# Two pairs of attention and GEGLU layers on one core: filling work given out by a running sum, and the second slot's gate moved from step 11 to step 9

## The chip, the cores and the metric

The kernel runs on one core of a Trainium2 chip. The metric is the time of one execution on the device in microseconds (us), as the median of several runs. The engines are named as in the profile: PE (TensorE, matrix products), DVE (VectorE), ACT (ScalarE), POOL (GpSimd) and SP (SyncE, which issues most transfers here).

## The reference

An input x of 2048 rows by 512 columns goes through four layers, each added to x: attention, feed-forward, attention, feed-forward. Cut to what matters:

```python
x = x + attention(layernorm(x)); x = x + ffn(layernorm(x))
x = x + attention(layernorm(x)); x = x + ffn(layernorm(x))

def attention(x):            # 32 heads of width 16, 4 segments of 512 rows, in order
    q, k, v = x @ wq, x @ wk, x @ wv            # each 512 x 512
    for s in range(4):
        p = softmax(q_s @ k_s.T / 4 + causal_mask)
        a_dot = p @ v_s
        a_mem = (phi(q_s) @ M) / (phi(q_s) @ z + 1e-6)   # phi(t) = t + 1 if t > 0, else exp(t)
        o_s = g * a_mem + (1 - g) * a_dot                 # g = sigmoid(beta), per head
        M = M + phi(k_s).T @ v_s;  z = z + phi(k_s).sum(0)
    return o @ wo

def ffn(x):                  # w_gate, w_up: 512 x 1792, w_down: 1792 x 512
    return (gelu(x @ w_gate) * (x @ w_up)) @ w_down
```

## The kernel before, in words

The work is cut into eight attention units (two attention layers of four segments each) and eight feed-forward units. The program runs through eight slots, k = 0 to 7. In slot k the softmax part of attention unit k is worked in 20 steps, t = 0 to 19 (the loop calls them steps; the title of the change calls them pairs). Around these steps lies everything else, as filling work for PE.

A step (function scores) does 4 or 8 small products of queries and keys (tile st in PSUM, two buffers, each holding two banks), then two exponentials on ACT (pt from st, 128 x 1024 each), then masks on POOL (line 368). Steps with t mod 5 equal to 1, 2 or 4 have 8 products, the others 4. The next step's products write the same two st buffers, so they wait for this step's exponentials. After steps with t mod 5 = 2 or 4 a block of 40 small products with v falls due one step later (function flush, tile ps_q, line 394); it reads the masked pt.

The filling of slot k is a list of items, each with a cost written by hand in us: 0.87 for four 512-wide products, 1.52 for seven of them, and so on. In slots 1 to 7 the list has two parts. The first (pre) is the memory part of unit k (den, four num, upd), the output projection wo of unit k-1 in four pieces (wo0 to wo3), the down projection of feed-forward unit k-2 in eight halves (d00, d01 to d30, d31), and the first half of the q and k projections of unit k+1 (q0, k0, q1, k1). After wo1 and after wo3 the layer norm of two row tiles each is started; it runs over DVE (add, statistics), POOL (lines 156 and 159: ve and rs), DVE again (xn, line 161) and SP (transposes of xn into xnT). Then comes the gate of feed-forward unit k-1: 56 products (tile psg, line 438) and seven Gelus on ACT, in one piece with no steps between. It needs all of xnT, and uses the st buffers. Before it ACT loads the table of the Gelu, and after it the table of the exponential. The second part (post) is the up projection in 14 items (u0 to u13, line 446), q2, k2, q3, k3 and the v projection v0 to v3 of unit k+1. Slot 0 has no gate: its list is its own v, q and k, the v, q and k of unit 1, upd, two loads and two layer norms. It alone cuts each step in two and runs filling also between the halves.

The orders of PE, ACT and SP are those in which the program is written. Those of DVE and POOL are set by a scheduler. All fillings, den and num too, and the flushes take their PSUM from one pool of four buffers (tag m). What q and k leave to do on ACT (an exponential e for phi) and v on ACT (a copy) is deferred until after the exponentials of the next step.

Before the change, the filling of a step is counted down: budget = remaining cost / remaining steps, items are run while less than the budget is spent, half of it (0.5) ahead of the flush and the rest behind it. An item that overshoots the budget is run whole. In the part ahead of the gate 1.7 us are held back (GATE_LEAD), and 1.7 us of the second part are run at once behind it (GATE_TAIL).

Of the kernel before, what the change touches and what calls it, by code (L numbers as in the profile page):

```python
# [31 lines left out]
STEPS = 4 * PAIRS  # L32
FLUSH_LAG = 1
G_STEP = 11
G_FIRST = 11
GATE_LEAD = 1.7
GATE_TAIL = 1.7
ST_BUFS = 2
# [4 lines left out]
def kernel(  # L43
# [39 lines left out]
    def load_x(sgi):  # L83
        nc.sync.dma_start(out=x_sb[:, TPS * sgi:TPS * (sgi + 1), :], in_=xv[:, TPS * sgi:TPS * (sgi + 1), :])

    def load_w(w_sb, w):
        nc.sync.dma_start(out=w_sb[:], in_=w.rearrange("(kt p) n -> p kt n", p=P))
# [11 lines left out]
                            fill=1.0, base=0, channel_multiplier=1)  # L99
# [3 lines left out]
                            fill=0.0, base=0, channel_multiplier=1)  # L103
    nc.gpsimd.affine_select(out=bd[:], in_=bd[:], pattern=[[16, 8], [0, 16]], compare_op=ALU.is_ge,
                            fill=0.0, base=15, channel_multiplier=-1)
# [17 lines left out]
    def late_constants():  # L123
        nc.vector.tensor_scalar(out=cden[:], in0=tmp_e[:], scalar1=1.0, scalar2=None, op0=ALU.add)
        for i in range(2):
            va = cst.tile([P, TPS, H, DH + 1], BF16, name=f"vaug{i}")
            nc.vector.tensor_copy(out=va[:, :, :, DH], in_=cden[:].unsqueeze(1).to_broadcast([P, TPS, H]))
            vaugs.append(va)
        nc.vector.tensor_scalar(out=tmp_e2[:], in0=tmp_e2[:], scalar1=1.0, scalar2=None, op0=ALU.add)
        nc.vector.reciprocal(out=gvec[:], in_=tmp_e2[:])  # L130
        for b in range(4):
            nc.vector.tensor_tensor(out=bdg[:, b, :].rearrange("p (h e) -> p h e", e=16),
                                    in0=bd[:].rearrange("p (h e) -> p h e", e=16),
                                    in1=gvec[:, 8 * b:8 * b + 8].unsqueeze(2).to_broadcast([P, 8, 16]),
                                    op=ALU.mult)
# [46 lines left out]
    def run_deferred():  # L182
        while deferred:
            deferred.pop(0)()
# [299 lines left out]
    fill = []  # L484
    clock = [0]

    def run_fill(budget):
        spent = 0.0
        while fill and spent < budget:
            c, fn = fill.pop(0)  # L490
            fn()
            spent += c
            while len(deferred) > 2:
                deferred.pop(0)()
        return spent

    def flush_due(force=False):
        while pending and (force or pending[0][0] <= clock[0]):
            _, u, b, par, pts = pending.pop(0)
            u.flush(b, par, pts)  # L500
            if (b, par) == (3, 1):
                u.turn()

    def merge(a, b):
        outl, na, nb = [], len(a), len(b)
        ia = ib = 0
        while ia < na or ib < nb:
            if ib >= nb or (ia < na and ia * nb <= ib * na):
                outl.append(a[ia]); ia += 1
            else:  # L510
                outl.append(b[ib]); ib += 1
        return outl

    with tc.manual_schedule(engines={ENG.PE, ENG.Activation, ENG.SP}):
        ln0 = LN(0)
        for j in range(TPS):
            ln0.stats(j)
        x0T = ln0.by_pe()
        late_constants()
        qk0, v0 = att[0].stage_a(lambda: x0T)  # L520
        for c, fn in qk0[:2]:
            fn()
            run_deferred()
        for i in range(1, NSEG):
            a_ln[i] = LN(TPS * i)

        def ln_items(i, with_stats):
            items = [(0.0, lambda j=j: a_ln[i].stats(j)) for j in range(TPS)] if with_stats else []
            return items + [(0.0, lambda: a_ln[i].by_dma())]

        for k in range(2 * NSEG):
            A = att[k]
            nxt_qk, nxt_v = [], []
            if k + 1 < 2 * NSEG:
                nxt_qk, nxt_v = att[k + 1].stage_a(lambda k=k: a_ln[k + 1].xnT)
            upd = A.mem_update() if A.s < NSEG - 1 else []
            if k == 0:
                pre = (v0 + qk0[2:4] + ln_items(1, True) + qk0[4:] + nxt_v + nxt_qk[0::2] + upd
                       + [(0.0, lambda: load_x(3)), (0.0, lambda: load_w(wd_sb, B_w_down))]
                       + ln_items(2, True) + nxt_qk[1::2])  # L540
                post, F, g_at = [], None, STEPS
            else:
                F = ffn[k - 1]
                f_ln = LN(F.tt0)
                wo_prev = att[k - 1].wo(f_ln)
                wo_prev = (wo_prev[:2] + [(0.0, lambda f_ln=f_ln: f_ln.by_dma(0, 2))] + wo_prev[2:]
                           + [(0.0, lambda f_ln=f_ln: f_ln.by_dma(2, 2))])
                pre = (A.mem() if A.s > 0 else []) + upd
                if k == 1:
                    pre += nxt_qk[:2] + wo_prev + nxt_qk[2:4]  # L550
                    g_at = G_FIRST
                else:
                    Fp, ln_d = ffn[k - 2], None
                    if Fp.lyr == 1:
                        ln_d = a_ln[NSEG + Fp.c] = LN(Fp.tt0)
                    down_prev = Fp.down(ln_d)
                    pre += down_prev[:4] + merge(wo_prev + down_prev[4:], nxt_qk[:4])
                    g_at = G_STEP
                post = merge(F.up(), nxt_qk[4:] + nxt_v)
                if k + 2 < 2 * NSEG:  # L560
                    post = merge(post, ln_items(k + 2, k + 2 < NSEG))
            fill[:] = pre
            for t in range(STEPS):
                if t == g_at:
                    run_fill(1e9)
                    run_deferred()
                    F.gate(f_ln.xnT)
                    fill[:] = post
                    run_fill(GATE_TAIL)
                left = (g_at if t < g_at else STEPS) - t  # L570
                if t < g_at <= STEPS - 1:
                    budget = max(0.0, sum(c for c, _ in fill) - GATE_LEAD) / left
                else:
                    budget = sum(c for c, _ in fill) / left
                budget -= 1e-6
                if k == 1 and 4 <= t < 8:
                    budget = max(budget, 1.74)
                if k == 0:
                    budget = max(budget, 1.0)
                    part = []  # L580
                    got = A.scores(t, between=lambda: part.append(run_fill(0.45 * budget)))
                    budget -= part[0]
                else:
                    got = A.scores(t)
                run_deferred()
                clock[0] += 1
                if got:
                    pending.append((clock[0] + FLUSH_LAG, A, *got))
                budget -= run_fill(0.5)
                flush_due()  # L590
                run_fill(budget)
            run_fill(1e9)


        F = ffn[-1]
        f_ln = LN(F.tt0)
        wo = att[-1].wo(f_ln)
        down_prev = ffn[-2].down(None)
        fill[:] = down_prev[:2]
        run_fill(1e9)  # L600
        flush_due(force=True)
        fill[:] = down_prev[2:5] + wo + down_prev[5:]
        run_fill(1e9)
        run_deferred()
        F.gate(f_ln.by_pe())
        for c, fn in F.up() + F.down(None):
            fn()
# [30 lines left out]
```

## Time and profile before

| | |
|---|---|
| median of 3 runs | 649.8 us (649.67 to 650.47) |
| the profiled execution | 648.93 us, span 647.2 us |
| mean granted PE clock | 0.965 |
| PE busy | 600.8 us (93%) |
| ACT busy | 426.2 us (66%) |
| DVE busy | 388.1 us (60%) |
| POOL busy | 221.4 us (34%) |

The span is the time from the first to the last instruction of the profile; 1.7 us of the execution lie outside it. Matmuls are pipelined and their ends are modelled, so starts are the firmer numbers. In the timeline a row reads: start, length, engine, line, operation, tile written<-tiles read, shape, count, and in brackets the idle time ahead and what ended it. The rows that matter stand in the prediction.

### The profile page before, as it was taken

To read this page: it belongs to the slowest core of one execution; us is meant where nothing else is said; L and a number is where in the kernel's file an instruction comes from. 1 tells how busy PE (TensorE), PEld (TensorE's weight loads), DVE (VectorE), ACT (ScalarE), POOL (GpSimd) and SP (SyncE) were. 2 spreads that over 40 slices of the span, in tenths; PEclk is the share of its full clock that TensorE was granted. 3 is DMA by queue.
4 is the path that set the end of the run, shared out by engine and by line. 5 is a ranking of instruction groups with operands and counts; after the bars stand their busy time and mean duration, and the time that the engine had idled before them with its cause. 6 is when DMAs were issued, how large, how long until landed. Compare 5 with 4: busy or idle time off the path is not lost.

```text
span 647.2 us, 14327 instructions
## 1 busy us (share of the span) xinstructions
PE 600.8 (93%) x5856; PEld 284.9 (44%) x5856; DVE 388.1 (60%) x917; ACT 426.2 (66%) x474; POOL 221.4 (34%) x505
## 2 busy tenths in 40 slices
PE   3997786999999999999999999999999999989997
PEld 1343543445444544444454454445444444434443
DVE  5897395467847568364756588386654546144352
ACT  2588785785767767675777858587676877572420
POOL 1434453143523445142432435133431445042000
PEclk9798595999999999998999999999999999999999
DMA  8945021021120012101130012210210012001001
GB/s 291 205 147 92 10 50 25 1 50 35 24 44 2 2 34 51 32 17 34 27 57 11 10 33 43 41 18 12 49 42 1 2 43 46 13 1 44 23 0 33
DMA packets 70578, 27.42 MB, mean 42 GB/s; under 512 B 61552, under 2 KB 69488, under 8 KB 70512
## 3 DMA queue, kind: packets, MB, share of 16 engines
q1 hardware_dynamic: 70368, 26.49, 18.1%
q8 instruction: 46, 0.75, 0.5%
q14 instruction: 20, 0.16, 0.1%
q10 hardware_dynamic: 144, 0.01, 0.0%
HBM read 9.71 MB, written 2.10 MB: 18 GB/s over the span
## 4 chain that ended last, share of the span: by engine, by line
PE 68%; ACT 12%; issue 8%; DVE 7%; POOL 3%; DMA 1%; SPq 0%; POOLq 0%; ACTq 0%
PE psg L438 15%; PE psu L446 13%; ACT pt L359 11%; PE psd L462 11%; PE st L352 9%; PE ps_q L394 7%; PE ps L206 5%; PE ps L247 4%; PE pso L419 2%; DMA x_sb<-in_A_x_dram 1%; DVE st L147 1%; POOL pt L368 1%; POOL rs L159 1%; DVE x_sb L422 1%; DVE xn L161 1%
## 5 line engine op out<-in xcount | busy, mean ns | idle before, releaser
L359 ACT ACTIVATE pt<-st 128x1024 bf16<-128x1024 f32 x320 | 310.4, 1024 | 107.3 <-PE st L352 103.5
L368 POOL TENSOR_SCALAR_AFFINE_SELECT pt<-pt 128x256 bf16<-128x256 bf16 (+1 forms) x448 | 195.5, 452 | 334.3 <-ACT pt L359 327.4
L449 DVE TENSOR_TENSOR gel<-gel,psu 128x512 bf16<-128x512 bf16 x112 | 76.3, 685 | 139.6 <-PE psu L446 136.2
L446 PE MATMUL psu<-xnT,wu_sb 128*128 128x512 bf16 x448 | 111.8, 380 | 0.0
L462 PE MATMUL psd<-wd_sb,gel 128*128 128x512 bf16 x448 | 105.1, 382 | 1.9 <-DVE x_sb L422 1.9
L438 PE MATMUL psg<-xnT,wg_sb 128*128 128x512 bf16 x448 | 100.4, 384 | 0.3
L440 ACT ACTIVATE gel<-psg 128x1024 bf16<-128x1024 f32 x56 | 57.3, 1024 | 47.9 <-PE psg L438 47.8
L394 PEld LDWEIGHTS <-pt 128*128 128x128 bf16 x2560 | 73.9, 97 | 18.1 <-POOL pt L368 3.8
L394 PE MATMUL ps_q<-vaug,pt 128*128 128x17 bf16 x2560 | 75.1, 171 | 3.5 <-POOL pt L368 3.5
L352 PE MATMUL st<-qfull,kmA 32*128 32x384 bf16 (+3 forms) x512 | 55.6, 313 | 17.0 <-ACT pt L359 13.2
L438 PEld LDWEIGHTS <-wg_sb 128*128 128x128 bf16 x448 | 43.8, 99 | 53.3 <-issue 3.7
L462 PEld LDWEIGHTS <-gel 128*128 128x128 bf16 x448 | 41.1, 98 | 54.7 <-issue 11.2
L446 PEld LDWEIGHTS <-wu_sb 128*128 128x128 bf16 x448 | 39.1, 97 | 49.0 <-issue 9.7
L352 PE MATMUL st<-qfull,kmB 32*128 32x128 bf16 (+3 forms) x512 | 48.4, 309 | 7.4 <-ACT pt L359 6.0
L147 DVE BATCH_NORM_STATS2 st<-x_sb 128x6 f32<-128x512 bf16 x64 | 43.3, 682 | 7.3 <-DMA x_sb<-in_A_x_dram 6.5
L352 PEld LDWEIGHTS <-kmA 32*128 32x128 bf16 x512 | 16.2, 93 | 70.8 <-issue 66.8
L466 DVE TENSOR_TENSOR x_sb<-x_sb,psd 128x512 bf16<-128x512 bf16 x32 | 21.9, 685 | 39.6 <-PE psd L462 39.5
L161 DVE TENSOR_SCALAR xn<-x_sb,mv,rs 128x512 bf16<-128x512 bf16 x64 | 28.6, 489 | 21.5 <-POOL rs L159 21.5
L247 PE MATMUL ps<-wv_sb,xnT 128*128 128x512 bf16 x128 | 35.6, 403 | 0.0
L206 PE MATMUL ps<-xnT,wq_sb 128*128 128x512 bf16 x128 | 33.9, 388 | 0.0
L206 PE MATMUL ps<-xnT,wk_sb 128*128 128x512 bf16 x128 | 33.9, 388 | 0.0
L419 PE MATMUL pso<-wo_sb,aT 128*128 128x512 bf16 x128 | 32.5, 381 | 0.3 <-DVE mv L148 0.3
(69 smaller groups left out, 461.3 us busy)
## 6 DMA issues: line engine op xcount, KB each, us to landing
out_dram<-x_sb SPq DMA_DIRECT2D x16, 128.0 KB, 1.7
wg_sb<-in_B_w_gate_dram SPq DMA_DIRECT2D x1, 1792.0 KB, 13.2
wu_sb<-in_B_w_up_dram SPq DMA_DIRECT2D x1, 1792.0 KB, 14.7
wd_sb<-in_B_w_down_dram SPq DMA_DIRECT2D x1, 1792.0 KB, 9.9
x_sb<-in_A_x_dram SPq DMA_DIRECT2D x3, 512.0 KB, 9.1
xnT<-xn SPq DMA_TRANSPOSE x56, 2.4
x_sb<-in_A_x_dram SPq DMA_DIRECT2D x4, 128.0 KB, 2.8
wq_sb<-in_A_wq_dram SPq DMA_DIRECT2D x1, 512.0 KB, 5.6
```

Of the source, the lines that this page charges most:

```text
L147: nc.vector.bn_stats(out=st6[:, 0, :], in_=x_sb[:, self.tt0 + j, :])
L206: nc.tensor.matmul(ps[:], lhsT=w[:, kt, b * P:(b + 1) * P], rhs=xnT[:, kt, :], start=(kt == 0), stop=(kt == KT - 1))
L247: nc.tensor.matmul(ps[:], lhsT=xnT[:, kt, j * P:(j + 1) * P], rhs=wv_sb[:, kt, :], start=(kt == 0), stop=(kt == KT - 1))
L352: nc.tensor.matmul(sts[j // 2][:, j % 2, c0:c0 + N], lhsT=kst[32 * j:32 * j + 32, b, P * ki:P * ki + P], rhs=self.qfull[32 * j:32 * j + 32 ...
L359: nc.scalar.activation(out=pt[:], in_=st[:], func=ACT.Exp, scale=SCALE)
L368: nc.gpsimd.affine_select(out=dv, in_=dv, pattern=[[0, n], [1, P]], compare_op=ALU.is_ge, fill=0.0, base=0, channel_multiplier=-1)
L394: nc.tensor.matmul(ps_q[:, qi, j, :], lhsT=two[j // 2][:, j % 2, cb:cb + P], rhs=self.vaug[:, ki, 8 * b + 2 * j + par, :], start=(cnt == 0 ...
L438: nc.tensor.matmul(psg[:, i, :], lhsT=wg_sb[:, kt, ft * P:(ft + 1) * P], rhs=xnT[:, kt, :], start=(kt == 0), stop=(kt == KT - 1))
L440: nc.scalar.activation(out=self.gel[:, 2 * f2:2 * f2 + 2, :], in_=psg[:], func=ACT.Gelu_apprx_tanh)
L446: nc.tensor.matmul(psu[:], lhsT=wu_sb[:, kt, ft * P:(ft + 1) * P], rhs=self.xnT[:, kt, :], start=(kt == 0), stop=(kt == KT - 1))
L449: nc.vector.tensor_tensor(out=g, in0=g, in1=psu[:], op=ALU.mult)
L462: nc.tensor.matmul(psd[:], lhsT=self.gel[:, ft, j * P:(j + 1) * P], rhs=wd_sb[:, ft, :], start=(ft == 0), stop=(ft == FT - 1))
```

## The change

It does two things. Filling is given out by a running sum: new_fill sets the sum to zero at the start of each part, and share says how far the sum may go by a point of a step: the part's whole cost times the share of its steps that have passed. An item is run when the sum with half of its cost is within that, so it is rounded to the nearest point instead of up. In slot 0 the two floors on the budget (1.0, which ran the list empty early) are replaced by shares that last to step 17 or 18. And in slot 1 the gate stands ahead of step 9 instead of step 11 (G_FIRST).

```diff
-G_FIRST = 11
+G_FIRST = 9
...
-    def run_fill(budget):
-        spent = 0.0
-        while fill and spent < budget:
+    spent = [0.0]
+
+    def run_fill(upto):
+        while fill and spent[0] + 0.5 * fill[0][0] <= upto:
             c, fn = fill.pop(0)
             fn()
-            spent += c
+            spent[0] += c
             while len(deferred) > 2:
                 deferred.pop(0)()
-        return spent
+
+    def new_fill(items):
+        run_fill(1e9)
+        fill[:] = items
+        spent[0] = 0.0
+        return sum(c for c, _ in items)
...
-            fill[:] = pre
+            total = new_fill(pre)
+            t0, n = 0, min(g_at, STEPS)
+            if F is not None:
+                total -= GATE_LEAD
             for t in range(STEPS):
                 if t == g_at:
                     run_fill(1e9)
                     run_deferred()
                     F.gate(f_ln.xnT)
-                    fill[:] = post
+                    total = new_fill(post) - GATE_TAIL
                     run_fill(GATE_TAIL)
-                left = (g_at if t < g_at else STEPS) - t
-                if t < g_at <= STEPS - 1:
-                    budget = max(0.0, sum(c for c, _ in fill) - GATE_LEAD) / left
-                else:
-                    budget = sum(c for c, _ in fill) / left
-                budget -= 1e-6
-                if k == 1 and 4 <= t < 8:
-                    budget = max(budget, 1.74)
+                    spent[0] -= GATE_TAIL
+                    t0, n = g_at, STEPS - g_at
+
+                def share(part):
+                    x = total * min(1.0, (t - t0 + part) / n)
+                    if k == 0:
+                        x = total * min(1.0, (t + 1 + part) / (n - 1))
+                    elif k == 1 and 4 <= t < 8:
+                        x = max(x, spent[0] + (0.9 if part < 1 else 1.0))
+                    return x
+
                 if k == 0:
-                    budget = max(budget, 1.0)
-                    part = []
-                    got = A.scores(t, between=lambda: part.append(run_fill(0.45 * budget)))
-                    budget -= part[0]
+                    got = A.scores(t, between=lambda: run_fill(share(0.5)))
                 else:
                     got = A.scores(t)
                 run_deferred()
                 ...
-                budget -= run_fill(0.5)
+                run_fill(share(0.5))
                 flush_due()
-                run_fill(budget)
+                run_fill(share(1.0))
```

The work itself, its tiles and the items' costs stay as they are; only the order changes. Three places show it.

ACT, from the fillings of slot 0 to the gate of slot 1. Here pt<-st are the exponentials of the steps, two to a step; e<-kf and e<-qfull are those that a k or a q item leaves behind; gel<-psg are the Gelus of the gate. Before:

```order
L237 ACTIVATE e<-kf 128x512 x2
L359 ACTIVATE pt<-st 128x1024 x2
L237 ACTIVATE e<-kf 128x512 x2
L359 ACTIVATE pt<-st 128x1024 x24
L222 ACTIVATE e<-qfull 128x512
L359 ACTIVATE pt<-st 128x1024 x2
L237 ACTIVATE e<-kf 128x512
L359 ACTIVATE pt<-st 128x1024 x6
L222 ACTIVATE e<-qfull 128x512
L237 ACTIVATE e<-kf 128x512
L359 ACTIVATE pt<-st 128x1024 x6
L440 ACT_TABLE_LOAD
```

Now:

```order
L237 ACTIVATE e<-kf 128x512
L359 ACTIVATE pt<-st 128x1024 x2
L237 ACTIVATE e<-kf 128x512
L359 ACTIVATE pt<-st 128x1024 x12
L222 ACTIVATE e<-qfull 128x512
L359 ACTIVATE pt<-st 128x1024 x2
L237 ACTIVATE e<-kf 128x512
L359 ACTIVATE pt<-st 128x1024 x4
L222 ACTIVATE e<-qfull 128x512
L359 ACTIVATE pt<-st 128x1024 x2
L237 ACTIVATE e<-kf 128x512
L440 ACT_TABLE_LOAD
```

The run of 24 exponentials with no item's exponential among them (twelve steps, from step 12 of slot 0 to step 3 of slot 1) shrinks to 12: k items now run until step 17 of slot 0. The gate's table load moves ahead by two steps.

PE, the last products ahead of the gate of slot 2 (psd is the down projection, ps_q the flush, psg the gate). Before:

```order
L394 LDWEIGHTS pt
L394 MATMUL ps_q<-vaug_165,pt 128x17
L394 LDWEIGHTS pt
L394 MATMUL ps_q<-vaug_165,pt 128x17
L438 LDWEIGHTS wg_sb
L438 MATMUL psg<-xnT,wg_sb 128x512
```

Now:

```order
L462 LDWEIGHTS gel
L462 MATMUL psd<-wd_sb,gel 128x512
L462 LDWEIGHTS gel
L462 MATMUL psd<-wd_sb,gel 128x512
L438 LDWEIGHTS wg_sb
L438 MATMUL psg<-xnT,wg_sb 128x512
```

Step 10 used to hold d31 and the flush. It now holds k1, the flush and d30, and d31 follows them when the rest of the list is run ahead of the gate. The same holds in slots 3 to 6 (without k1 in 3 and 4), and in slot 7.

PE, the end of the filling of step 11 in slot 2, the first step behind its gate (psu is the up projection, ps with wk_sb the k2 item, st the next step's products). Before:

```order
L206 LDWEIGHTS wk_sb
L206 MATMUL ps<-xnT,wk_sb 128x512
L446 LDWEIGHTS wu_sb
L446 MATMUL psu<-xnT,wu_sb 128x512
L446 LDWEIGHTS wu_sb
L446 MATMUL psu<-xnT,wu_sb 128x512
L446 LDWEIGHTS wu_sb
L446 MATMUL psu<-xnT,wu_sb 128x512
L446 LDWEIGHTS wu_sb
L446 MATMUL psu<-xnT,wu_sb 128x512
L352 LDWEIGHTS kmA
```

Now:

```order
L206 LDWEIGHTS wk_sb
L206 MATMUL ps<-xnT,wk_sb 128x512
L206 LDWEIGHTS wk_sb
L206 MATMUL ps<-xnT,wk_sb 128x512
L206 LDWEIGHTS wk_sb
L206 MATMUL ps<-xnT,wk_sb 128x512
L206 LDWEIGHTS wk_sb
L206 MATMUL ps<-xnT,wk_sb 128x512
L352 LDWEIGHTS kmA
```

The step's filling was u1, k2, u2 and is now u1, k2; u2 goes to step 12. Counted so through the whole order, the items of slot 2 stand like this (F is a flush, the number ahead of a colon is the step):

```
before 0: den num0 F num1 num2 num3 upd   1: d00 d01   2: d10 d11   3: wo0 F q0   4: wo1 k0
       5: wo2 F wo3   6: q1 d20   7: d21   8: k1 F   9: d30   10: d31 F   gate u0 q2
       11: u1 k2 u2   12: u3 q3 u4   13: u5 F k3   14: u6 u7   15: v0 F u8   16: v1 u9
       17: u10 v2   18: u11 F u12   19: v3 u13
now    0: den num0 num1 F num2 num3   1: upd d00   2: d01   3: F d10   4: d11
       5: wo0 F q0   6: wo1 k0 wo2   7: wo3 q1   8: F d20   9: d21   10: k1 F d30   d31 gate u0 q2
       11: u1 k2   12: u2 u3   13: q3 u4 F u5   14: k3 u6   15: u7 F v0   16: u8 v1
       17: u9 u10 v2   18: u11 F u12   19: v3 u13
```

In slot 1 they are, up to the gate, before: 0: den num0 F num1, 1: num2 num3 upd, 2: q0, 3: k0 F, 4: wo0 wo1, 5: wo2 F wo3, 6: q1 k1, 7: none, 8: F, 9: none, 10: F, gate. Now: 0: den F num0 num1, 1: num2 num3, 2: upd, 3: F q0, 4: k0 wo0, 5: wo1 F wo2, 6: wo3 q1, 7: k1, 8: F, gate.

8 lines of the change are left out of this document (4 added, 4 removed).

## The prediction

> **What bounds the kernel now.** I read the page's first lines, then the trace by stage, then the timeline of PE and ACT in single steps. The page first:
>
> ```profile
> PE 600.8 (93%) x5856; PEld 284.9 (44%) x5856; DVE 388.1 (60%) x917; ACT 426.2 (66%) x474; POOL 221.4 (34%) x505
> ```
>
> PE sets the pace, and its work stays the same. So the change is worth what it does to PE's waits, slot by slot. The next rows are stretches of the span: length, then busy time of PE, PEld, DVE, ACT and POOL, then the granted PE clock. They are the filled steps of slot 0, its bare steps 12 to 19, slot 1 up to its gate, that gate, slot 1 behind it, slot 2 and slot 7.
>
> ```profile
> 17.60:53.50 35.90, 35.88 (x344) 15.21 (x344) 31.76 (x85) 26.80 (x32) 15.73 (x34) 0.90 0.79 171
> 53.50:74.00 20.50, 12.61 (x191) 6.29 (x188) 8.57 (x26) 17.66 (x21) 9.85 (x23) 0.65 0.13 27
> 74.00:107.00 33.00, 25.34 (x365) 14.34 (x365) 27.21 (x72) 25.02 (x28) 17.07 (x39) 0.76 0.20 41
> 107.00:121.00 14.00, 14.00 (x57) 5.98 (x57) 1.57 (x5) 6.14 (x6) 0.55 (x2) 0.86 0.00 0
> 121.00:148.70 27.70, 27.16 (x271) 12.15 (x270) 19.14 (x42) 22.70 (x27) 10.49 (x24) 1.00 0.15 30
> 148.70:222.80 74.10, 72.71 (x747) 35.04 (x747) 48.46 (x112) 52.11 (x58) 27.47 (x63) 1.00 0.11 23
> 519.90:586.10 66.20, 61.35 (x662) 29.76 (x662) 29.75 (x62) 47.03 (x49) 25.27 (x59) 1.00 0.11 25
> ```
>
> Slot 0 first has PE full and ACT three quarters busy, then ACT full and PE at 61%: filling there is badly spread. Slots 2 to 7 have little to win.
>
> What a step needs is seen in slot 3, PE and then ACT. Step 2 starts at 231.53, its filling (one half of a down projection) at 231.86; step 3 starts at 233.47, its filling at 234.34.
>
> ```profile
> 231.53 0.29 PE L352 MATMUL st<-qfull,kmA 32*128 32x256 bf16 x4
> 231.86 1.68 PE L462 MATMUL psd<-wd_sb,gel 128*128 128x512 bf16 x7
> 233.47 0.93 PE L352 MATMUL st<-qfull,kmB 32*128 32x512 bf16 x4
> 234.34 1.04 PE L419 MATMUL pso<-wo_sb,aT 128*128 128x512 bf16 x4
> 235.21 1.15 PE L394 MATMUL ps_q<-vaug,pt 128*128 128x17 bf16 x40
> 236.21 1.02 PE L206 MATMUL ps<-xnT,wq_sb 128*128 128x512 bf16 x4
> 237.17 0.40 PE L352 MATMUL st<-qfull,kmB 32*128 32x384 bf16 x8
> ...
> 232.02 3.88 ACT L359 ACTIVATE pt<-st 128x1024 bf16<-128x1024 f32 x4 [1.50 <-PE st L352]
> ```
>
> From start to start, a step's own products take 0.33, a half of d 1.61, an item of four products 0.87 (0.96 as the last of a step), a flush 1.00. From filling to filling lie 234.34 - 231.86 = 2.48, though 1.61 + 0.33 = 1.94 would do: the second pair of products waits for the last exponential. **The rule of a step**: it lasts its filling plus 0.33, but at least 2.49. A filling under 2.16 leaves PE waiting for the difference: one half of d 0.54, two items (1.83) 0.33, one item 1.2. Filling above 2.16 saves nothing elsewhere. Where a wait lets exponentials of a 4-product step start early, the next floor is 0.1 to 0.4 lower.
>
> Behind a gate the floor is higher (slot 3, step 11, ACT last):
>
> ```profile
> 270.01 1.04 PE L446 MATMUL psu<-xnT,wu_sb 128*128 128x512 bf16 x4
> 270.88 1.03 PE L206 MATMUL ps<-xnT,wk_sb 128*128 128x512 bf16 x4
> 271.74 1.03 PE L446 MATMUL psu<-xnT,wu_sb 128*128 128x512 bf16 x4
> 272.70 0.28 PE L352 MATMUL st<-qfull,kmA 32*128 32x256 bf16 x2
> 273.79 1.04 PE L446 MATMUL psu<-xnT,wu_sb 128*128 128x512 bf16 x4
> ...
> 270.18 1.28 ACT L359 ACT_TABLE_LOAD   x1 [1.10 <-PE st L352]
> ```
>
> The table load stretches it to 273.79 - 270.01 = 3.78; three items (2.69) leave a wait of 0.76, two (1.83) leave 1.61.
>
> **The change, slots 2 to 7.** Slot 2 by the rule. Before, the thin steps are 4 (0.33), 7 (0.55), 8 (0.13), 9 (0.45), 11 (0.76), 14 (0.32), 16 (0.32), 17 (0.26) and 19 (0.33): 3.45. Now they are 2 (0.54), 4 (0.54), 7 (0.32), 9 (0.55), 11 (1.61), 12 (0.26), 14, 16 and 19 (0.97): 4.79, or 1.35 more. The reason is in the lists: step 10 and what follows it up to the gate hold 5.0 (k1, F, d30, d31) where 2.16 covers the exponentials, and step 13 holds 3.7; this surplus is missing in steps 2 and 11. Slot 6 has the same lists, slot 5 comes to 1.9 (its q items leave no exponential, which moves the floors), slots 3 and 4 to 1.6 each (steps 1, 2 and 4 thin, step 3 with 4.1). Slot 7: steps 7 and 11 fall to one item, which costs 0.6 and 0.9 more; +1.5. Sum 9.5.
>
> Against it stand waits for PSUM buffers, which the cluster wo2, F, wo3, q1, d20 causes now, since DVE is late with the add for wo2:
>
> ```profile
> PE psd L462 <- DVE x_sb L422: 1.9, 4, 0.7
> ```
>
> With d20 a step behind q1 and F between them these four should go: -1.9. In slot 4, d00 now stands behind step 1 and so behind less of its wait: -0.4 (my estimate, from the 0.33 of a step's products). Sum for slots 2 to 7: **+7.2**, between +5 (a third of the new waits absorbed) and +9.5.
>
> **Slot 0.** These are PE in step 7, then ACT with an item's exponential in step 8, then ACT in bare steps, PE's flush there, and the step behind it:
>
> ```profile
> 42.05 0.28 PE L352 MATMUL st<-qfull,kmA 32*128 32x256 bf16 x2
> 42.38 1.04 PE L206 MATMUL ps<-xnT,wq_sb 128*128 128x512 bf16 x4
> 43.35 0.39 PE L352 MATMUL st<-qfull,kmB 32*128 32x512 bf16 x2
> ...
> 43.47 0.62 ACT L222 ACTIVATE e<-qfull 128x512 bf16<-128x512 bf16 x1
> 43.99 2.17 ACT L359 ACTIVATE pt<-st 128x1024 bf16<-128x1024 f32 x2
> ...
> 57.78 3.75 ACT L359 ACTIVATE pt<-st 128x1024 bf16<-128x1024 f32 x4
> 62.18 3.77 ACT L359 ACTIVATE pt<-st 128x1024 bf16<-128x1024 f32 x4 [0.66 <-PE st L352]
> ...
> 64.71 1.24 PE L394 MATMUL ps_q<-vaug,pt 128*128 128x17 bf16 x40
> 65.88 0.73 PE L352 MATMUL st<-qfull,kmA 32*128 32x384 bf16 x8
> ```
>
> Half a step with an item costs PE 0.33 + 0.97, so two items make a step of 2.58. ACT alone needs 1.83 for a step (four exponentials in 3.75), 0.52 for an item's exponential (43.47 to 43.99), and 0.66 where a flush holds up the next products. Steps 2 to 19 now take 48.1 (from 25.9, where the first two steps end, to 74.0). After the change most hold one item: with a flush 0.65 + 0.97 + 1.08 = 2.7 (steps 3, 8, 13), 2.6 (10), with two items and a flush 3.6 (5, 15), bare with a flush 2.5 (18): 20.3 together. Step 9 (two items) takes 2.6, step 14 (upd) 2.1. The other nine are ACT's, 1.83: 16.5. That is 41.5; eleven item exponentials add 5.7 if none falls into ACT's idle time and nothing if all do; most run in a step with a flush or just ahead of one, where ACT has 0.3 to 1.2 to spare. I take 1.1, near that end, so 42.6 and **-5.5**, between -6.6 and -3.5. Loads and layer norms move with the list, but SP runs ahead of PE: x and w_down are wanted only in slots 1 and 2, and v0 of unit 1 moves from step 5 to 7, behind its transposes.
>
> **Slot 1.** The path to its gate, PE, then POOL, then SP, and last, from the chain of work, the gate of slot 2:
>
> ```profile
> 90.58 1.02 PE L419 MATMUL pso<-wo_sb,aT 128*128 128x512 bf16 x4
> 102.53 0.97 PE L394 MATMUL ps_q<-vaug,pt 128*128 128x17 bf16 x30
> 106.38 0.63 PE L394 MATMUL ps_q<-vaug,pt 128*128 128x17 bf16 x10 [2.88 <-POOL pt L368]
> ...
> 104.58 0.23 POOL L156 TENSOR_SCALAR ve<-mv 128x4 f32<-128x4 f32 x1 [2.71 <-DVE mv L148]
> ...
> 93.43 7.33 SPq L167 DMA_TRANSPOSE xnT<-xn  x4
> ...
> 183.16 12.10 PE psg L438 x56
> ```
>
> wo3 ends at 91.5; the last transpose of xnT is issued by 100.8, and the page gives 2.4 from issue to landing, so xnT is whole near 102. The gate starts at 107.0 because the flush ahead of it waits for masks, behind a layer norm on POOL. Now that flush comes behind the gate. But wo3 moves to step 6, whose filling starts by the rule 16.3 behind the slot's start; wo3 ends at 17.2, and with the same 10.5 for add, statistics, POOL, DVE and SP the gate can start at 27.7 to 28.2 (33.0 before). PE is ready at 23 and idles five, more than the 2.88 that leave the clock low now (0.86 granted over this gate, 14.0 instead of the 12.1 of slot 2); so 14.0 again. Behind the gate 11 steps instead of 9 share the same items. To the 27.7 come the flush (1.1), the products of two steps (0.7) and the waits, by the rule 5.1 instead of 1.9, most in steps 9 (1.61), 11 and 17 (1.2 each): 32.7. Sum 28.0 + 14.0 + 32.7 = 74.7, against 33.0 + 14.0 + 27.7 = 74.7. For the start I add **+0.3**, between -2 and +3.
>
> The start hangs on PE's clock. In the bare tail of slot 0 PE is 61% busy and the granted clock is 0.65; slot 7, 93% busy, keeps 1.00. The longest idle time in that tail is this row's 2.02:
>
> ```profile
> 58.83 0.39 PE L352 MATMUL st<-qfull,kmB 32*128 32x512 bf16 x2 [2.02 <-ACT pt L359]
> ```
>
>  The new tail has one item in steps 16 and 17 (1.6 of 2.1 busy) and bare steps 18 and 19. I take it as warm; a cold one costs slot 1 about 1.5, which lies in the range. The Trainium skill (TensorE: Matmul & The Clock Gate, Why this matters for your kernels) warns only of idle gaps above about 3 us; by that the tail stays warm for certain and slot 1 keeps its 74.7. The trace disagrees: it shows the low clock behind shorter gaps.
>
> **Sum.** -5.5 + 0.3 + 7.2 = +2.0 on the profiled 648.9, 650.9. That execution lies 0.9 under the median; on 649.8 it is **651.8 us**.
>
> **The rivals.**
> - *Slot 0 pays for the rest.* If ACT's idle time takes all item exponentials (-6.6) and a third of the new waits in slots 2 to 7 is absorbed (+5), the sum is -1.3 and 648.5 to 651.1 is reached with any mixture. For it: the rule ignores how an early step helps the next but one. Against it: on the lists of before it gives 3.45 for slot 2, about what PE's starts there show. 0.31, of which 0.04 faster than that.
> - *The gate of slot 1 doesn't wait.* If DVE works wo3's add at once, xnT is there when PE is (23 instead of 28), PE stays warm, and 5.0 + 1.9 go: 645. It decides below about 6 us from wo3 to the landing. Against it: 10.5 now, with q1 and k1 ahead of it on DVE as before. 0.13.
> - *Later gates start to wait.* In slots 2 to 6 wo3 moves from step 5 to 7, the gate stays at 11; by the rule 12 us are left between them. If DVE's backlog takes 2 us more than now, each of five gates waits 0.5 to 1: up to 656. 0.10.
> - That lasting filling isn't had is partly so: d31 still piles up ahead of each gate.
>
> **Numbers.** My forecast has 0.46. About 0.2% (1.3 us) can be told from no change. Slower 0.46 + 0.10 = 0.56, the same 0.27, faster 0.04 + 0.13 = 0.17. The range leaves out most of the second rival and the end of the third: 648.3 to 655.2.
>
> **What would show it.** Slot 0 ends near 68.5 with no bare stretch but steps 18 and 19; slot 1's gate starts 28 behind the slot's start, after PE idled on SP's transposes; steps 12 of slots 2 to 7 wait 1.6 for ACT; slots 2 to 6 last 1 to 2 us longer each. It is wrong if slot 0 stays above 71, if that gate starts by 25, or if slots 2 to 6 keep their lengths.

## The result, and the profile after

The changed kernel takes 666.58 us (median of four runs, 666.11 to 667.07), where the kernel before took 649.73 beside it: a ratio of 1.0262, 95% interval [1.0243, 1.0281]. The forecast was 651.8, range 648.3 to 655.2. The direction was right, the size was not: the profiled span went from 647.2 to 664.6, 17.4 us more where 2.0 were forecast.

The page's first lines, after (busy time, share of the span and instructions of each engine, then the granted PE clock in forty slices):

```profile
PE 601.0 (90%) x5776; PEld 285.9 (43%) x5856; DVE 393.9 (59%) x917; ACT 425.6 (64%) x474; POOL 223.9 (34%) x505
...
PEclk9896787899999999997999999999999999998999
```

By these lines PE is busy as long as before (600.8). But 80 of 5856 matmul records are missing in this trace, and products at a low clock count as busy too, so how much of the 17.4 us is waiting and how much is slower work can't be read here; lengths are taken from starts. The stretches of the span, after (length, then busy time and number of instructions of PE, PEld, DVE, ACT and POOL, then the granted clock, and last the share and GB/s of the DMA engines): slot 0 up to step 13, its steps 14 and 15, its tail, slot 1 up to its gate, that gate, slot 1 behind it, slot 2, slot 7.

```profile
17.60:53.00 35.40, 31.99 (x335) 13.52 (x341) 28.30 (x69) 29.20 (x34) 18.84 (x40) 0.95 0.64 172
53.00:62.60 9.60, 9.38 (x126) 5.24 (x123) 6.69 (x22) 5.99 (x8) 3.17 (x8) 0.50 0.31 32
62.60:71.00 8.40, 5.65 (x75) 2.52 (x69) 7.63 (x21) 8.09 (x11) 3.84 (x8) 0.91 0.23 47
71.00:102.60 31.60, 23.38 (x310) 12.44 (x311) 24.06 (x64) 21.49 (x24) 14.88 (x32) 0.72 0.21 43
102.60:116.90 14.30, 13.79 (x53) 5.93 (x56) 3.45 (x11) 6.14 (x6) 1.28 (x2) 0.83 0.05 10
116.90:150.90 34.00, 31.13 (x318) 13.94 (x320) 20.55 (x45) 26.39 (x31) 12.68 (x30) 0.95 0.12 25
150.90:227.30 76.40, 72.56 (x735) 35.21 (x744) 49.24 (x112) 52.21 (x58) 28.02 (x63) 1.00 0.14 22
534.50:601.00 66.50, 59.64 (x601) 28.18 (x610) 28.75 (x59) 46.95 (x49) 25.47 (x59) 0.98 0.11 25
```

Two things stand out. In slot 0 there is now a stretch of 9.6 us in which PE is full (9.38) at half the clock (0.50), and slot 1 ahead of its gate runs at 0.72. And slot 2 lasts 76.4 instead of 74.1 at full clock. By slots, from the starts of the first products of each:

| us | before | after | difference | forecast |
|---|---|---|---|---|
| slot 0 | 56.3 | 53.4 | -2.9 | -5.5 |
| slot 1 | 74.7 | 79.9 | +5.2 | +0.3 |
| slots 2 to 6 | 371.2 | 383.6 | +12.4 | |
| slot 7 and the end | 127.3 | 130.0 | +2.7 | |
| slots 2 to 7 together | 498.5 | 513.6 | +15.1 | +7.2 |

Each column is one profile. In the profiles of the experiments below slots 2 to 6 last 371.2 to 373.2 with the old counting and 383.6 to 386.1 with the running sum (no deferral), so differences of 1 or 2 us there are not firm.

Of slots 2 to 6, first PE's longest waits before the change, then those of PE and ACT after it (what waited, for whom; us in total, times, longest):

```profile
PE st L352 <- ACT pt L359: 2.5, 6, 0.5
```

```profile
PE st L352 <- ACT pt L359: 13.5, 26, 1.4
...
ACT e L222 <- DVE qfull L218: 9.4, 4, 2.8
...
ACT e L237 <- DVE kf L229: 2.6, 3, 1.5
...
PE psd L462 <- DVE x_sb L422: 0.7, 3, 0.2
```

The two ACT rows have no counterpart in these slots before. ACT takes its work in order, and the exponential e of a q or k item stands ahead of a later step's exponentials. If DVE's cast of that item is late, ACT waits, and the step's exponentials behind it are late too. One such place, slot 2, after: ACT, then DVE, then PE.

```profile
174.98 1.94 ACT L359 ACTIVATE pt<-st 128x1024 bf16<-128x1024 f32 x2 [0.22 <-PE st L352]
178.95 0.63 ACT L222 ACTIVATE e<-qfull 128x512 bf16<-128x512 bf16 x1 [2.03 <-DVE qfull L218]
179.49 3.75 ACT L359 ACTIVATE pt<-st 128x1024 bf16<-128x1024 f32 x4
...
175.79 1.27 DVE L422 TENSOR_TENSOR x_sb<-x_sb,pso 128x512 bf16<-128x512 bf16 x2
176.99 1.27 DVE L147 BATCH_NORM_STATS2 st<-x_sb 128x6 f32<-128x512 bf16 x2
178.26 0.65 DVE L218 CAST qfull<-ps 128x512 bf16<-128x512 f32 x1
...
180.54 0.39 PE L352 MATMUL st<-qfull,kmA 32*128 32x512 bf16 x2 [0.41 <-ACT pt L359]
181.46 0.39 PE L352 MATMUL st<-qfull,kmA 32*128 32x512 bf16 x2 [0.52 <-ACT pt L359]
```

DVE works the adds and statistics of wo2 and wo3 first and casts q1 only at 178.26. ACT idles 2.03 for it, and PE's next step pays. The Trainium skill (Perfetto Trace Analysis, Tensor Engine Instruction) says that ACT and DVE are strict first in, first out; these rows agree.

### The profile page after: what moved, and what is told of

The parts are those of the page before. It is cut to its first block, busy times and chain, and to the rows that moved or that the text cites. A ratio compares the mean times of both kernels' runs of the same rounds, so it can differ in the third digit from the quotient of the medians.

```text
span 664.6 us, 14238 instructions
## 1 busy us (share of the span) xinstructions
PE 601.0 (90%) x5776; PEld 285.9 (43%) x5856; DVE 393.9 (59%) x917; ACT 425.6 (64%) x474; POOL 223.9 (34%) x505
## 3 DMA queue, kind: packets, MB, share of 16 engines
q1 hardware_dynamic: 70368, 26.49, 17.2%
## 4 chain that ended last, share of the span: by engine, by line
PE 69%; ACT 11%; DVE 9%; issue 7%; DMA 2%; POOL 2%; SPq 0%; POOLq 0%; ACTq 0%; DVEq 0%
PE psg L438 15%; PE psu L446 14%; ACT pt L359 10%; PE psd L462 10%; PE st L352 9%; PE ps_q L394 9%; PE ps L206 5%; PE ps L247 3%; DVE st L147 2%; PE pso L419 2%; DVE x_sb L422 1%; DMA x_sb<-in_A_x_dram 1%; DVE xn L161 1%; POOL rs L159 1%; PE psn L280 1%
## 5 line engine op out<-in xcount | busy, mean ns | idle before, releaser
L368 POOL TENSOR_SCALAR_AFFINE_SELECT pt<-pt 128x256 bf16<-128x256 bf16 (+1 forms) x448 | 197.7, 456 | 321.7 <-ACT pt L359 313.0
L462 PE MATMUL psd<-wd_sb,gel 128*128 128x512 bf16 x421 | 103.5, 384 | 2.8 <-issue 0.8
L394 PEld LDWEIGHTS <-pt 128*128 128x128 bf16 x2560 | 72.4, 96 | 14.1 <-issue 5.3
L438 PEld LDWEIGHTS <-wg_sb 128*128 128x128 bf16 x448 | 44.3, 99 | 61.1 <-issue 10.3
L352 PE MATMUL st<-qfull,kmB 32*128 32x384 bf16 (+3 forms) x512 | 49.0, 306 | 6.3 <-ACT pt L359 4.9
L206 PE MATMUL ps<-xnT,wk_sb 128*128 128x512 bf16 x126 | 36.3, 411 | 0.3 <-issue 0.2
L247 PE MATMUL ps<-wv_sb,xnT 128*128 128x512 bf16 x120 | 33.8, 394 | 0.4
```

The lines of the kernel that those rows point to most:

```text
L206: nc.tensor.matmul(ps[:], lhsT=w[:, kt, b * P:(b + 1) * P], rhs=xnT[:, kt, :], start=(kt == 0), stop=(kt == KT - 1))
L247: nc.tensor.matmul(ps[:], lhsT=xnT[:, kt, j * P:(j + 1) * P], rhs=wv_sb[:, kt, :], start=(kt == 0), stop=(kt == KT - 1))
L352: nc.tensor.matmul(sts[j // 2][:, j % 2, c0:c0 + N], lhsT=kst[32 * j:32 * j + 32, b, P * ki:P * ki + P], rhs=self.qfull[32 * j:32 * j + 32 ...
L368: nc.gpsimd.affine_select(out=dv, in_=dv, pattern=[[0, n], [1, P]], compare_op=ALU.is_ge, fill=0.0, base=0, channel_multiplier=-1)
L394: nc.tensor.matmul(ps_q[:, qi, j, :], lhsT=two[j // 2][:, j % 2, cb:cb + P], rhs=self.vaug[:, ki, 8 * b + 2 * j + par, :], start=(cnt == 0 ...
L438: nc.tensor.matmul(psg[:, i, :], lhsT=wg_sb[:, kt, ft * P:(ft + 1) * P], rhs=xnT[:, kt, :], start=(kt == 0), stop=(kt == KT - 1))
```

## Experiments: which part of the change costs

Four kernels, each with one part. The gate of slot 1 at step 9, with the counting of before:

```diff
-G_FIRST = 11
+G_FIRST = 9
```

> The old counting down of the filling everywhere; only the gate of slot 1 stands ahead of step 9. By the slots of the two profiles the change lost 5.2 us in slot 1 and 15.2 in slots 2 to 7, and won 2.9 in slot 0. Theory A (the loss is made by the running sum, step by step): xnT can't be whole before 28 us into the slot, so the gate comes 5 us earlier than at step 11, and two more steps behind it cost about the same; 648 to 652. Rival B (the early gate is what upsets the kernel, since PE idles and runs at half clock behind it): 655 or more.

Measured 649.65, ratio 0.9994 [0.9967, 1.0021]: no difference. The running sum in all slots, with the gate of slot 1 left at step 11 (G_FIRST = 11 in the changed kernel):

> The running sum everywhere, but the gate of slot 1 stays ahead of step 11. Theory A: slots 2 to 7 lose their 15 us as with the whole change, slot 0 wins 3, slot 1 lies between its old and new length; 660 to 667. Rival B (the early gate is the cause): 646 to 652.

Measured 660.98, ratio 1.0172 [1.014, 1.0204]. Then the running sum in slot 0 alone, and in slots 2 to 7 alone (the other slots keep the old loop, the gate of slot 1 stays at 11):

```diff
+NEW_SLOTS = (0,)                      # or (2, 3, 4, 5, 6, 7)
...
+            if k not in NEW_SLOTS:    # here the loop of before
...
```

> The running sum in slot 0 alone; all other slots as before, gate at step 11. Theory A: slot 0 wins its 2.9 us and slot 1 stays within 1 of its old length; 646 to 648. Rival C (spreading the filling of slot 0 leaves PE thinly busy, so the half clock moves into the loaded start of slot 1 and takes the gain back): 649 to 653.

> The running sum in slots 2 to 7 alone; slots 0 and 1 as before. Theory A: each of slots 2 to 6 lasts 2.1 to 3.0 us longer and slot 7 2.8 us, as in the profile of the whole change; 663 to 666. My prediction's own sum for these slots was 7.2: 657. Rival D (these slots suffer from what slots 0 and 1 hand on to them): below 655.

Measured 646.09, ratio 0.9942 [0.9922, 0.9962], and 664.26, ratio 1.0235 [1.0192, 1.0278]. So the running sum pays in slot 0 and costs in slots 2 to 7, whatever is done ahead of them. The gate costs nothing by itself, but 5.6 us together with the running sum (661.0 to 666.6). The first products of the gate of slot 1 show why; with the running sum and the gate at 11 first, then the whole change:

```profile
102.51 0.59 PE L438 MATMUL psg<-xnT,wg_sb 128*128 128x512 bf16 x1 [0.22 <-DMA xnT<-xn]
```

```profile
90.74 1.04 PE L419 MATMUL pso<-wo_sb,aT 128*128 128x512 bf16 x4
...
102.84 0.59 PE L438 MATMUL psg<-xnT,wg_sb 128*128 128x512 bf16 x1 [6.06 <-DMA xnT<-xn]
```

The transposes of xnT land 31.8 behind the slot's start in both (starts at 70.76 and 71.03). Put ahead of step 9 the gate starts no earlier; PE waits 6.06 and has two more steps to do behind it. With the old counting wo3 stands one step earlier, and the gate at step 9 starts 28.6 behind the slot's start (102.76 - 74.17) instead of 33.1, so there it wins ahead about what it loses behind.

## Experiments: slots 2 to 7

To take ACT's waits for DVE away without changing PE's order, the exponential of a q or k item was deferred by one step more in slots 1 to 7:

```diff
-    def run_deferred():
-        while deferred:
-            deferred.pop(0)()
+    def run_deferred(due=False):      # due in slots 1 to 7
+        hold = [f for f in deferred if due and getattr(f, "born", -1) >= clock[0]]
+        now = [f for f in deferred if f not in hold]
+        deferred[:] = hold
+        for f in now: f()
```

With it up to six of these exponentials may wait at a time, where it was two. First on the running sum in slots 2 to 7 alone, then on the kernel before, then on the whole change:

> The running sum in slots 2 to 7 as in the run with it alone there (664.3 us), but in slots 1 to 7 the exponential that a q or k item leaves for ACT is deferred by one step more, so that ACT no longer stops for DVE's cast of that item. Theory (the rule of a step was right, and what it lacked is ACT waiting in order for DVE): 4 to 6 us come back, 658 to 660, about what the rule alone gives (650 + 9.5). Rival (DVE's backlog holds PE through PSUM buffers, ACT's wait is only its sign): no change, 663 to 665.

> The kernel before, only with the exponentials of q and k items deferred by one step more in slots 1 to 7. Theory: before the change ACT seldom waits for DVE, so 647 to 650. Rival: ACT waits for DVE as much before as after, and 4 or more go, under 646.

> The whole change, and the exponentials of q and k items deferred by one step more in slots 1 to 7. The same deferral took 9.3 us from the running sum in slots 2 to 7 alone (664.3 to 655.0) and about 7 from the kernel before. Theory (ACT's waits for DVE cost the changed kernel only a few us more than the kernel before): 656 to 659, still slower than before by 1% or more. Rival (ACT's waits for DVE are the whole of what the prediction missed): 652 or less.

Measured 654.99, ratio 1.0088 [1.0051, 1.0124]; 642.04, ratio 0.9891 [0.9842, 0.994]; 658.76, ratio 1.0131 [1.01, 1.0162]. The first fell further than expected. The second went to the rival in its time: the kernel before gains 4 us in slot 1 and 3.6 in slots 2 to 6 (371.2 to 367.6). But not for the rival's reason, since ACT doesn't wait for casts in slots 2 to 6 there. Of the 3.6 there, 1.9 are PE's four waits for PSUM buffers, which are gone, and about 1 is a low clock in slot 4 (0.66 from 298 to 303) that the run with deferral didn't have; in slot 1 the flushes hardly wait for masks any more (3.5 to 0.4). The third is as expected: deferral takes 5.7 from slots 2 to 6 of the changed kernel (383.6 to 377.9). ACT's waits for q's casts are gone there, but three for k's casts are left, in step 10 of slots 3, 4 and 5 just ahead of the gate:

```profile
ACT e L239 <- DVE kf L231: 5.9, 3, 2.4
```

The gates behind them start without a wait of PE and last 12.1 like the others. So late casts cost both kernels, the changed one some 2 us more. Between the two with deferral 10.3 are left in slots 2 to 6, where the rule of a step gave 8.0. In slots 2, 3, 5 and 6, which run at 1.00 in both, it is 6.7, and the terms of the rule for these four add up to 6.2.

The rule itself was tested with lists by hand in slots 2 to 6, which leave hardly a filling under 2.16 and put four items behind the gate. Slot 0 has the running sum, the gate of slot 1 stays at 11. Slot 2 (names as in the lists above, num0 as n0, wo0 as w0, LN a layer norm):

```text
0: den n0 n1 F n2 n3   1: upd d00   2: d01 q0   3: F d10   4: w0 d11   5: w1 LN F w2   6: w3 LN d20
7: d21 k0   8: F d30   9: d31 q1   10: k1 F   gate u0 LN q2   11: u1 k2 u2 u3   12: q3 u4 u5
13: k3 F   14: u6 u7 v0   15: u8 F   16: v1 u9   17: u10 v2 u11   18: u12 F   19: v3 u13
```

> Slot 0 by the running sum (646.1 us alone), gate of slot 1 at step 11, and in slots 2 to 6 a list written by hand of which items stand in which step: next to no filling under 2.16, four items in the step behind the gate, nothing else changed. Theory (a step costs what its filling lacks to 2.16, or to 3.45 behind a gate): the waits of the old counting, 3.45 in slot 2 and as much in the others, fall to about 1.5, so 8 to 10 us less than 646.1, 636 to 640. Rival (thin steps aren't what costs; clusters on DVE or the old gaps lie elsewhere): 645 to 648.

> As the kernel with the list by hand, and the exponentials of q and k items deferred by one step more in slots 1 to 7. Theory: where the lists keep DVE ahead there is little for it to take away: 0 to 3 us less than the list by hand. Rival (ACT waits for DVE everywhere): 4 or more less.

Measured 641.83, ratio 0.9885 [0.9833, 0.9938], and with deferral 636.23, ratio 0.9807 [0.9754, 0.9859]. Slots 2, 3, 4 and 6 last 72.1, 71.3, 74.2 and 71.5 with the list, 1.3 to 2.6 less than before, as the rule says. Slot 5 lasts 77.7, 3 more than before, and that is why the first kernel came out above 640 and missed its range. Its gate, PE with the list by hand, with ACT's rows from just ahead:

```profile
400.74 0.63 ACT L246 ACTIVATE e<-kf 128x512 bf16<-128x512 bf16 x1 [2.31 <-DVE kf L238]
...
401.39 1.28 ACT L449 ACT_TABLE_LOAD   x1
...
403.76 2.60 PE L447 MATMUL psg<-xnT,wg_sb 128*128 128x512 bf16 x8 [2.43 <-ACT gel L449]
```

k1's exponential waits 2.31 for DVE, the table load and the Gelus stand behind it, and the gate stops after its two buffers are full. It lasts 16.4 instead of 12.1: the wait of 2.43, and behind it a low clock (0.63 from 404 to 407). Deferral takes 3.2 of slot 5, and 3.8 from slot 1; slots 2, 3, 4 and 6 it changes by 0.9 at most, and none of them gains. That total, 5.6, is the rival's size, but it comes from two places, not from everywhere.

## Experiments: slots 0 and 1

To keep PE busy without changing its work, products that nobody reads were put where it otherwise waits (0.2 us each):

```diff
+    def warm(n):
+        ps = psp.tile([P, L], F32, tag="m", bufs=M_BUFS)
+        for i in range(n):
+            nc.tensor.matmul(ps[:], lhsT=wk_sb[:, 0, 0:P], rhs=wk_sb[:, 1, :], start=(i == 0), stop=(i == n - 1))
...
                 run_fill(share(1.0))
+                if (k, t) in WARM:   # (0,10): 2, (0,11): 5, (0,12): 3, (0,16) to (0,18): 3, (0,19): 4
+                    warm(WARM[k, t]) # and (1,1): 3, (1,7): 3, (1,8): 24
```

> The whole change, and extra products that nobody reads (0.2 us each) where PE otherwise waits: steps 10, 11, 12 and 16 to 19 of slot 0, steps 1, 7 and 8 of slot 1. Theory (PE's waits there make the chip grant half the clock, and the half clock then falls on loaded steps of slots 0 and 1): the granted clock stays at 1.00 in slot 0 behind step 12 and for most of slot 1, slot 0 loses 2 to 3.5 us, slot 1 loses 3 to 5, 658 to 662. Rival (the low clock has another cause than PE's waits, or the order alone sets the length): the clock falls as before and the time stays at 666 to 669.

> The whole change, with the extra products in slot 0 alone. Theory (the tail of slot 0 is what makes the clock low in slot 1): slot 0 52, slot 1 75 to 76, 662 to 664. Rival (slot 1's own waits, the one at its gate above all, keep the clock low by themselves): slot 1 stays at 78 to 80, 664.5 to 667.

Measured 659.67, ratio 1.0147 [1.0113, 1.0181], and, with the products in slot 0 alone, 663.04, ratio 1.0232 [1.0203, 1.0261]: the first theory each time, though the split of the first run was off (slot 0 lost 1.3, slot 1 7.2). The stretches from 53.0 to the end of slot 0, slot 1 up to its gate, the gate and what follows, with the products in both slots:

```profile
53.00:62.60 9.60, 9.38 (x155) 5.44 (x154) 9.31 (x29) 8.41 (x10) 4.16 (x11) 1.00 0.31 23
62.60:68.90 6.30, 6.07 (x72) 2.73 (x70) 5.89 (x16) 6.30 (x10) 3.40 (x7) 1.00 0.31 62
68.90:97.00 28.10, 26.48 (x343) 13.94 (x343) 23.80 (x64) 21.36 (x24) 14.74 (x32) 1.00 0.25 50
97.00:109.00 12.00, 12.00 (x57) 5.46 (x56) 3.07 (x10) 6.14 (x6) 1.28 (x2) 1.00 0.04 8
109.00:141.60 32.60, 29.89 (x321) 13.56 (x319) 20.54 (x45) 26.38 (x31) 12.66 (x30) 1.00 0.13 26
```

The clock is 1.00 throughout. PE does more and the stretch is over sooner: slot 0 ends at 68.9 (71.0), slot 1 lasts 72.7 (79.9). With the products in slot 0 alone, slot 0 ends at 68.4, and slot 1 lasts 75.5: 4.4 of its 7.2 hang on the tail of slot 0. The other 2.8 are won only with products in slot 1's own waits: 1.1 up to the gate and 1.6 in the gate. With the products in slot 0 alone the wait at the gate is still there, and the clock is low again around it (slot 1 up to its gate, the first products of the gate, the gate):

```profile
68.40:98.20 29.80, 21.30 (x311) 11.73 (x314) 24.45 (x65) 21.37 (x24) 14.75 (x32) 0.87 0.25 50
97.48 0.58 PE L438 MATMUL psg<-xnT,wg_sb 128*128 128x512 bf16 x1 [5.50 <-DMA xnT<-xn]
98.20:111.20 13.00, 12.86 (x54) 5.61 (x55) 2.50 (x9) 6.14 (x6) 1.28 (x2) 0.90 0.00 0
```

The counterpart, such products in steps 12 to 19 of slot 0 (2 or 6 each) and 7 to 9 of slot 1 of the kernel before:

> The kernel before with extra products that nobody reads in steps 12 to 19 of slot 0 and 7 to 9 of slot 1: the counterpart of the same addition to the changed kernel, which took 7 us from it, all in slots 0 and 1 (53.4 to 52.1, 79.9 to 72.7). Theory (the low clock costs the changed kernel's slot 1 more than the kernel before, since it falls on loaded steps): here slots 0 and 1 lose 2 to 4 together, 645.5 to 648. Rival (the low clock costs both the same, and slot 1 is longer because of its order alone): 6 or more go, under 644.

Measured 650.65, ratio 1.0017 [0.9981, 1.0052]; the total fits neither. The clock still dropped, behind the waits of step 12, and the six products of step 14 then took 2.68 where those of step 16 take 1.40. From there on the tail ran at 1.00:

```profile
59.00:62.00 3.00, 2.58 (x52) 1.48 (x53) 1.23 (x4) 2.15 (x4) 1.64 (x3) 0.83 0.44 87
62.00:65.00 3.00, 3.00 (x22) 1.02 (x21) 0.00 (x0) 1.94 (x3) 1.54 (x4) 0.60 0.00 0
65.00:74.00 9.00, 8.37 (x121) 4.09 (x120) 1.36 (x4) 8.10 (x9) 4.44 (x10) 1.00 0.01 2
```

So slot 0 grew from 56.3 to 57.2, and slot 1 kept its 74.7 behind a warm end of the tail, where that of the changed kernel lost 4.4. This speaks for the first theory in slot 1, though it isn't shown: slot 1 still ran at 0.87 ahead of its gate, and runs of this kernel lie 8 us apart (644.74 at a mean clock of 0.989, 652.80 the longest), so what the low clock costs the kernel before in all stays open.

## A version that beats both

The list by hand with wo0 to wo3 a step earlier, deferral, and slot 1 by a list too, with its gate at step 9; then with extra products that nobody reads in slots 0 and 1; then with slot 1 by the old counting and its gate at 11, and extra products there in steps 7 to 9:

> The list by hand with deferral (636.2 us), now also for slot 1 with its gate at step 9, and with wo0 to wo3 a step earlier, right behind the transposes of aT. Theory (in slot 1 the path wo3, layer norm, transposes sets when a gate can start, and an early gate pays only if that path is early too; slot 5 of the list by hand lost up to 4 at its gate on the same path): slot 1 66 to 68 instead of 70.9, slot 5 72 to 73 instead of 74.6, 628 to 633. Rival (an early gate in slot 1 costs behind it what it saves ahead): 635 to 637.

> As the list by hand in slots 1 to 6, and the extra products that nobody reads in steps 10, 11, 12 and 16 to 19 of slot 0 and 6 and 7 of slot 1. Theory of the clock: 3 to 6 us less than that kernel. Rival: the same time or up to 2 more.

> The list by hand with deferral and extra products (631.4 us), but slot 1 again by the old counting with its gate at step 11, which lasted 70.9 where the early gate took 73.3. Theory (an early gate doesn't pay while DVE and the masks behind it set when it can start): 628 to 630. Rival (the early gate isn't what made slot 1 longer): 631 to 633.

Measured 634.20, ratio 0.9749 [0.9722, 0.9777]; 631.42, ratio 0.9729 [0.9692, 0.9767]; 627.00, ratio 0.9673 [0.964, 0.9706]. The first missed: slot 1 took 74.1, 3 more than with the gate at 11, though slot 5 came to 72.0. (Slot 5's loss was put on the transposes in that expectation; the rows above show that it was ACT.) The intervals of the first two overlap, so the extra products alone are unclear there. The last lost its early gate and won 5.6 in slot 1 (73.3 to 67.7); but the list of slot 1 and its extra products changed along with the gate, so which of the three won isn't separated. Its slots 2 to 6 last 71.2 to 72.0. Slot 1 ahead of the gate, and slot 2, in this version:

```profile
69.45:94.00 24.55, 21.57 (x325) 12.11 (x329) 21.28 (x53) 19.94 (x23) 14.26 (x32) 1.00 0.25 51
...
137.20:208.90 71.70, 70.50 (x736) 35.29 (x747) 49.06 (x112) 52.57 (x58) 27.73 (x63) 1.00 0.12 24
```

## Why the prediction was wrong

Of the 15.4 us that the span missed the forecast by, 2.6 lie in slot 0, 4.9 in slot 1 and 7.9 in slots 2 to 7.

*Slot 0, -5.5 forecast, -2.9 measured.* The counting of steps held; what failed is that every step is priced at the full clock. "I take it as warm" speaks of steps 16 to 19 only. The clock fell to 0.50 just ahead of 53.0 and stayed there over steps 14 and 15, where now upd, two k items and a flush lay. They took 3.06 and 5.50, where the text had 2.1 and 3.6; with the extra products in slot 0 alone they took 1.93 and 3.72. With the clock kept up slot 0 ends at 68.4 and 68.9 in the two runs, where the text had 68.5, and lasts 51.0 and 52.1 (50.8 by the forecast). The range was too narrow as well: 5.7 for the item exponentials, which the text allows for, reaches to -0.9, and it stopped at -3.5.

*Slot 1, +0.3 forecast, +5.2 measured.* Here "I take it as warm" failed, and the price beside it, for which the text has no working, was mis-sized: "a cold one costs slot 1 about 1.5". It cost 4.4. At a clock of 0.72 wo3 ended 20.6 behind the slot's start instead of 17.2. The path from there to the gate took 11 as expected, PE waited on the transposes as expected, and the gate and the steps behind it lasted 14.3 and 33.8. With the tail kept warm and slot 1 left alone the terms come out near those of the text: gate 29.1 behind the slot's start (28.0), 13.7 for the gate (14.0), 32.7 behind it (32.7). With all of it warm the gate starts at 27.9 and lasts 12.1. The mean granted clock hardly changed (0.965 to 0.961); that the old order suffered less from it because it lay on bare steps there (12.61 of 20.50 busy) and lies on filled ones here (9.38 of 9.60) is argued from these rows, not shown.

*Slots 2 to 7, +7.2 forecast, +15.1 measured.* The rule of a step was nearly right, and the step that failed is the one on what DVE's lateness would do. (The slots' terms as printed add up to 9.3, not 9.5, and 7.8 of it for slots 2 to 6. Slot 5 was given for its own a term on the ground that "its q items leave no exponential"; in the trace before they leave four there, and it is slot 3 where they leave none.) Slots 2 and 6, which have the same lists and ran at 1.00 in both profiles, show where the miss lies. From the gate to the slot's end the rule gives 0.85 more, and 0.86 were measured (27.67 to 28.53). From the slot's start to the gate it gives 0.5, and 1.45 were measured (34.33 to 35.78); with deferral on both sides it is 0.7 (33.87 to 34.57). So behind the gate all is as forecast. PE, then ACT, slot 2, after:

```profile
200.93 1.04 PE L446 MATMUL psu<-xnT,wu_sb 128*128 128x512 bf16 x4
201.80 1.03 PE L206 MATMUL ps<-xnT,wk_sb 128*128 128x512 bf16 x4
203.47 0.28 PE L352 MATMUL st<-qfull,kmA 32*128 32x256 bf16 x2 [0.64 <-ACT pt L359]
204.38 0.28 PE L352 MATMUL st<-qfull,kmA 32*128 32x256 bf16 x2 [0.63 <-ACT pt L359]
204.71 1.90 PE L446 MATMUL psu<-xnT,wu_sb 128*128 128x512 bf16 x7
...
201.10 1.28 ACT L359 ACT_TABLE_LOAD   x1 [1.09 <-PE st L352]
202.39 1.94 ACT L359 ACTIVATE pt<-st 128x1024 bf16<-128x1024 f32 x2
```

From filling to filling lie 204.71 - 200.93 = 3.78, and two items fill 1.83 of it, as in the text. What failed is "With d20 a step behind q1 and F between them these four should go: -1.9". Those four waits for PSUM did shrink, to 0.7, but DVE was late as before, and the debt moved: from PE's wait for a buffer to ACT's wait for a cast, 12.0 us in the rows above. Deferral, which removes PE's form and half of ACT's, is worth 3.6 before and 5.7 after; so the term is about +2 and not -1.9, and no firmer than the spread of the profiles. The text had weighed only who waits for DVE on PE. Slot 7 and the end took 2.7 instead of 1.5; 0.8 of that is an item of step 18 at a low clock (599.28 to 600.96, where four products take 0.87). With the running sum and the gate of slot 1 at step 11, and with the extra products in both slots, they last 128.8, which is the forecast. The low clock, after:

```profile
599.28 1.89 PE L446 MATMUL psu<-xnT,wu_sb 128*128 128x512 bf16 x4
600.96 1.26 PE L394 MATMUL ps_q<-vaug,pt 128*128 128x17 bf16 x40
...
597.80:603.00 5.20, 4.57 (x51) 2.18 (x51) 2.06 (x4) 2.75 (x4) 2.09 (x4) 0.67 0.00 0
```

*The rivals.* None came. "The gate of slot 1 doesn't wait" had a wait of 6.06 against it; "Later gates start to wait" found the gate of slot 2 at 12.1 and with no wait ahead of it, as in slots 3 to 6; "Slot 0 pays for the rest" would have needed a warm tail and a third of the waits absorbed. A cold tail had been put into the range at 1.5; ACT waiting in its order for DVE stood in none of them. The direction was right for the reason given, the thin steps of slots 2 to 7, which alone outweigh what slot 0 won.

## What to carry to other kernels

Floors per step on the bounding engine give a good estimate at one clock only: where a reordering fills steps that idled, ask first which loaded steps will be run at the low clock, and price those at about double (2.68 against 1.40 for six products here). When one engine waits for a late one (DVE here), moving that wait away need not gain anything, and didn't here, where DVE came no earlier; look for the next in-order queue that waits for it. One step more between an item and the exponential that follows it was worth 1.1% in the kernel before (ratio 0.9891); the running sum in the one slot where it helps gave 0.6% (0.9942), and the two intervals just overlap.

## What the runs showed of the hardware

The low clock doesn't need one long gap. In the changed kernel it began just ahead of 53.0, behind this stretch:

```profile
47.00:53.00 6.00, 4.45 (x46) 1.66 (x45) 4.71 (x11) 5.73 (x8) 2.81 (x6) 0.98 1.21 314
```

PE was busy 4.45 of 6.00 us there, its only wait was 1.55, and half the clock was then granted for 9.6 us in which PE was busy 98%. Two, five and three more products in steps 10, 11 and 12 were enough to keep 1.00 there and over the next 9.6 us. With them in slot 0 alone:

```profile
47.00:53.00 6.00, 6.00 (x35) 1.86 (x33) 3.97 (x9) 5.73 (x8) 2.81 (x6) 1.00 1.53 302
```

The Trainium skill (TensorE: Matmul & The Clock Gate) has two places on this. Its section "Why this matters for your kernels", used in the prediction, warns of gaps above about 3 us; this trace goes the other way, with 1.55. Its section "A second HAM failure mode: psum-queue depth-cycling" tells of a kernel in which frequent short idles between groups of products make the clock swing. The bare tail of slot 0 in the kernel before agrees with that (12.61 of 20.50 us busy, no wait above 2.02, a clock of 0.65); the stretch above, with its single wait, is covered by neither.
